# One shared PSUM pool of four double banks, score runs of up to three steps, and zero matmuls in the early gaps

## The chip, the cores and the metric

The kernel runs on one core of a Trainium2 chip. The metric is the device time of one execution in microseconds (us), median of several runs. A timed run is about 1.7 us longer than the span on its profile page.

Names of the engines: PE is TensorE (PEld its weight loads), DVE VectorE, ACT ScalarE, POOL GpSimd, SP SyncE. PSUM, into which PE writes, is used here as eight banks of 2 KiB per partition; "one bank" is 512 fp32 columns.

## The reference

Block-sparse attention (4 batches, 8 heads, 768 positions, head size 64; the mask has global blocks, a window and three random blocks per query block) is followed by a feed-forward layer with a gated activation.

```python
scores = scale * np.matmul(q, k.transpose(0, 1, 3, 2))
scores = np.where(mask, scores, -1000000000.0)
attn = np.exp(scores - max); attn = attn / sum
x = (attn @ v) as (3072, 512)
h = x @ w_in                                  # (3072, 2048)
g = h * (1.0 / (1.0 + np.exp(-beta * h)))
return g @ w_out                              # (3072, 512)
```

## The kernel before

All buffers are fixed tiles, allocated once. The order in which the instructions are issued comes from a scheduler in the kernel (`order_of`), which walks the work as nodes with modelled durations and hands out buffers. PSUM is split: two score buffers of two banks each, four one-bank buffers for all else.

```python
SLOTS = {..., "et": 15, "xst": 7, "t_sb": 5, "g": 2, "osb": 2, "sc": 2, "mm": 4}
T = {
    "sc": many(psum, "sc", [P, 2, 512], FP32),     # 2 tiles of 2 banks: scores
    "mm": many(psum, "mm", [P, 512], FP32),        # 4 tiles of 1 bank: everything else
    ...
def at(buf):
    return T[buf.pool][buf.slot]
```

A score step ("sc") is a group of 64-row matmuls that fills both banks of an `sc` tile; one exp on ACT then reads both, and DVE multiplies by the mask. The feed-forward works on units of one bank: "hp" is four matmuls into one `mm` bank, "th" a tanh on ACT that reads the bank, and "gm" a DVE operation that reads the tanh and the bank again.

```python
hb, tb = Buf("mm"), Buf("t_sb")
def hp(f=f, hb=hb):
    for c in range(NPAIR):                          # 4 matmuls of 512 columns
        nc.tensor.matmul(at(hb)[:, 0:n], lhsT=w_in_sb[:, c, f * P:(f + 1) * P],
                         rhs=xT_sb[:, c, t0:t0 + n], start=(c == 0), stop=(c == NPAIR - 1))
def th(eng, ...):
    nc.scalar.activation(out=at(tb)[:, 0:n], in_=at(hb)[:, 0:n], func=AF.Tanh, ...)
def gm(eng, ...):
    nc.vector.scalar_tensor_tensor(out=at(gb)[:, f, 0:n], in0=at(tb)[:, 0:n],
                                   scalar=1.0, in1=at(hb)[:, 0:n], op0=ALU.add, op1=ALU.mult)
...
seq = order_of(nodes, {...}, SLOTS)
with tc.manual_schedule():
    for n in seq:
        n.emit(...)
```

The kernel fixes the order; the semaphores that keep the engines apart are placed by the programming layer beneath it.

The softmax here doesn't subtract the row's maximum and nothing guards it: scores larger than these inputs give would overflow.

Of the kernel before, what the change touches and what calls it, by code (L numbers as in the profile page):

```python
# [23 lines left out]
class Node:  # L24


    def __init__(self, kind, eng, dur, lat, emit, deps=(), take=(), use=(), moved=0,
# [10 lines left out]
        self.start = self.done = self.on = None  # L38


BIAS = {"av": 39, "beta": 625, "cast": 183, "dma": -860, "ex": 395, "gm": -151, "hp": 34,
        "load": 1245, "lone sc": 160, "mask": -541, "mk": 266, "next sc": -48, "norm": 134,
        "op": 45, "op on": 85, "osb": 304, "sc": -79, "spread": 28, "th": 302, "turn": -1220,
        "turn cp": 47, "weights": 444, "x cp": 29, "x turn": -13}

W_GATE = (3, "k")
SLACK = 1500.0
AHEAD = 3
HOP = 60.0
SWITCH = 100.0  # L50
RATE = {"SP": 305.0, "POOL": 410.0}
# [2 lines left out]
SHARED = 42.0  # L54


def order_of(nodes, free, slots):

    free = dict(free)
    give = {p: [(0.0, s) for s in range(n)] for p, n in slots.items()}  # L60
    rows = 128
    wire = {"SP": 0.0, "POOL": 0.0}
    port = {"DVE": 0.0, "POOL": 0.0}
    left, after, at_dep = {}, {}, {}
    todo = []
    for n in nodes:
        left[n] = len(n.deps)
        at_dep[n] = n.at
        for d, x in n.deps:
            after.setdefault(d, []).append((n, x))  # L70
        if not n.deps:
            todo.append(n)
    out = []
    while todo:
        best = None
        for n in todo:
            ready = at_dep[n]
            want = {}
            for b in n.take:
                want[b.pool] = want.get(b.pool, 0) + 1  # L80
            ok = True
            for p, c in want.items():
                if len(give[p]) < c:
                    ok = False
                    break
                ready = max(ready, sorted(give[p])[c - 1][0])
            if not ok:
                continue
            for e in n.eng:
                n_start = max(ready, free[e])  # L90
                if n.port and e in port:
                    n_start = max(n_start, port["POOL" if e == "DVE" else "DVE"])
                bias = BIAS[n.kind]
                if n.rows == 64:
                    if rows == 64:
                        bias += BIAS["next sc"]
                    elif sum(t <= n_start for t, _ in give["sc"]) < 2:
                        bias += BIAS["lone sc"]
                key = (n_start + n.dur[e] - min(n.dur.values()) + bias, n.place)
                if best is None or key < best[0]:  # L100
                    best = (key, n, e, n_start)
        if best is None:
            raise RuntimeError("no node can start")
        _, n, e, start = best
        if e == "PE" and n.rows != rows:
            start, rows = start + SWITCH, n.rows
        n.on, n.start = e, start
        free[e] = start + n.dur[e]
        if n.port and e in port:
            port[e] = free[e]  # L110
        if n.moved:
            other = "POOL" if e == "SP" else "SP"
            t, rest, rate = max(wire[e], start + DMA_FIRST[e]), n.moved, RATE[e]
            if e == "SP" and wire[other] > t:
                both = min(rest, (wire[other] - t) * SHARED)
                wire[other] += both / RATE[other]
                t, rest = t + both / SHARED, rest - both
            wire[e] = t + rest / rate
            n.done = wire[e] + DMA_LAST
        else:  # L120
            n.done = free[e] + n.tail
        for b in n.take:
            t, b.slot = min(give[b.pool])
            give[b.pool].remove((t, b.slot))
        for b in n.use:
            b.users -= 1
            b.end = max(b.end, n.done)
            if b.users == 0:
                give[b.pool].append((b.end + HOP, b.slot))
        todo.remove(n)  # L130
        out.append(n)
        for m, x in after.get(n, ()):
            at_dep[m] = max(at_dep[m], n.done + HOP + x)
            left[m] -= 1
            if left[m] == 0:
                todo.append(m)
    if len(out) < len(nodes):
        raise RuntimeError("some nodes never become ready")
    return out


@with_exitstack
def kernel(
# [11 lines left out]
    nc = tc.nc  # L155
# [14 lines left out]
    VW = D + 2  # L170
    Q1 = 256

    SLOTS = {"st_k": 3, "st_q": 6, "st_v": 4, "s16_k": 4, "s16_q": 2, "set": 4, "va": 5,
             "et": 15, "xst": 7, "recip": 6, "t_sb": 5, "g": 2, "osb": 2, "sc": 2, "mm": 4}

    persist = ctx.enter_context(tc.tile_pool(name="persist", bufs=1))
    psum = ctx.enter_context(tc.tile_pool(name="psum", bufs=1, space=bass.MemoryType.PSUM))
# [1 line left out]
    def many(pool, tag, shape, dtype):  # L179
        return [pool.tile(shape, dtype, name=f"{tag}_{i}") for i in range(SLOTS[tag])]  # L180

    T = {
        "sc": many(psum, "sc", [P, 2, 512], FP32),
        "mm": many(psum, "mm", [P, 512], FP32),
        "et": many(persist, "et", [P, 2, 512], FP16),
        "xst": many(persist, "xst", [P, 4, 2, D], FP16),
        "recip": many(persist, "recip", [P, 2, 2, 1], FP32),
# [10 lines left out]
        T[f"s16_{nm}"] = many(persist, f"s16_{nm}", [P, 2 * NC * D], FP16)  # L198

    def at(buf):  # L200
        return T[buf.pool][buf.slot]

    identity = persist.tile([P, P], FP16, name="identity")
# [157 lines left out]
    def by_chunk(s16, lo, hi):  # L361
        return at(s16)[:, lo * P:hi * P].rearrange("p (c h d) -> p h c d", h=2, d=D)

    def add_load(nm, x, st, lo, hi, gate):
        b, j = pairs[x]
        src = {"k": k, "q": q, "v": v}[nm]

        def load():
            hg = src[b, 2 * j:2 * j + 2].rearrange("h (g p c) d -> p (h g) (c d)", g=NG, p=P)
            o = at(st).rearrange("p h (g c) -> p (h g) c", g=NG)  # L370
            if hi - lo == NC:
                nc.sync.dma_start(out=o, in_=hg)
            else:
                for g in range(lo // CG, hi // CG):
                    nc.sync.dma_start(out=o[:, g::NG], in_=hg[:, g::NG])
        deps = [(d, -1e9) for d in last_load + begin]
        kw = {"take": [st]}
        if gate is not None:
            def shut():
                nc.gpsimd.tensor_copy(out=at(st)[0:1, 0, lo * D:lo * D + 1],  # L380
                                      in_=w_out_sb[0:1, gate * 8, 0:1])
            deps.append(add("weights", "POOL", 600, 50, shut, deps=[w_out_of[gate]], take=[st]))
            kw = {"use": [st]}
        last_load[:] = [add("load", "SP", 500 if hi - lo in (NC, CG) else 1000, 0, load, deps=deps,
                             moved=68000 * (hi - lo) + (500000 if x == 0 and nm == "v" else 0),
                             **kw)]
        return last_load[0]

    def add_cast(x, nm, st, dst, lo, hi, load):
        w = (hi - lo) * P  # L390

        def cast(eng):
# [3 lines left out]
              in_=src)  # L396
        return add("cast", ("DVE", "POOL"), {"DVE": 60 + 0.53 * w, "POOL": 50 + 0.94 * w}, 90, cast,
                   deps=[(load, SLACK if x >= NPAIR else 4000 if lo and x == 3 else 0)],
                   take=[dst], use=[st], port=True)

    def add_half(x, nm, kq, lo, hi, first, gate):

        i = "kq".index(nm)
        w = (hi - lo) * P
        st, s16 = Buf(f"st_{nm}"), Buf(f"s16_{nm}")
        load = add_load(nm, x, st, lo, hi, gate)
        if x < NPAIR and lo == 0:
            loads[x, nm] = st, load
        c = add_cast(x, nm, st, s16, lo, hi, load)
        if x >= N_PE_TURN:  # L410
            def turn():
                nc.sync.dma_start_transpose(
# [18 lines left out]
    def add_prep(x, gates=(None, None, None)):  # L431
        kq, va, st = Buf("set"), Buf("va"), Buf("st_v")
        hi = Q1 // P if x < NPAIR else NC
        tk = add_half(x, "k", kq, 0, NC, None, gates[0])
        tq = add_half(x, "q", kq, 0, hi, tk, gates[1])
        lv = add_load("v", x, st, 0, NC, gates[2])
        cv = add_cast(x, "v", st, va, 0, NC, lv)
        prep[x] = {"kq": kq, "va": va, "k": tk, "q": tq, "q on": tq, "v": cv}
        if x < NPAIR:
            loads[x, "v"] = st, lv  # L440

# [6 lines left out]
    def tile_steps(x, q0, n):  # L448
# [5 lines left out]
        for kc0 in range(0, NC, kn):  # L454
# [19 lines left out]
            def mk(eng, et=et, kc0=kc0):  # L474
# [3 lines left out]
                    [P, 2 * CG * kn, w])  # L478
                nc.vector.tensor_tensor(out=e, in0=e, in1=m, op=ALU.mult)  # L479

            steps.append((x, q0, sc, et, mm, ex, mk,
                          [mask_of[g] for g in range(q0 // (CG * P), (q0 + n) // (CG * P))]))
        return steps, ets

    sc_of = {}

    def add_step(step, unit):
        x, q0, sc, et, mm, ex, mk, masks = step
        r = prep[x]
        g = add("sc", "PE", 218, 180, mm, deps=[(r["k"], SLACK if x >= N_PE_TURN else 0),  # L490
                      (r["q"] if q0 == 0 else r["q on"], SLACK if x >= N_PE_TURN else 0)],
                take=[sc], use=[r["kq"]], rows=64)
        sc_of.setdefault(unit, g)
# [136 lines left out]
    for i, (b, q0, n) in enumerate(tiles):  # L630
# [12 lines left out]
        while gi < len(moe) and moe[gi][0] + moe[gi][1] <= upto:  # L643
            add_moe(*moe[gi], gi)
            gi += 1

    seq = order_of(nodes, {"PE": 3900.0, "ACT": 3950.0, "DVE": 2800.0, "POOL": 3350.0,
                           "SP": 800.0}, SLOTS)

    with tc.manual_schedule():  # L650
        emit_first()
        for n in seq:
            if n.on in ("ACT", "DVE", "POOL") and n.emit.__code__.co_argcount > n_default(n.emit):
                n.emit(n.on)
            else:
                n.emit()
# [34 lines left out]
```

## Time and profile before

| | before |
|---|---|
| median of 3 runs | 280.38 us (280.29 to 280.6) |
| the profiled run | 281.79 us (span 280.1) |
| PE busy | 265.3 us, 95% |
| first hp matmul; second hp tile; last matmul | 33.61; 63.16; 276.05 us |

These lines are from the page of the kernel before: busy time by engine, the PE and clock rows of the forty slices, the chain of waits, and three groups. In the names, `et` is the exp of the scores, `va` the values, `xst` and `xT_sb` the attention output before and after it is turned (transposed), `t_sb` the tanh, `g` the gated activation, `osb` a piece of the result. A group's columns are its busy time and the mean ns of one instruction, then the engine's idle time before those instructions and what ended most of it.

```profile
PE 265.3 (95%) x2455; PEld 139.5 (50%) x2455; DVE 209.5 (75%) x424; ACT 212.9 (76%) x281; POOL 28.0 (10%) x45
PE   4597899999999999999999999999999999999994
PEclk9997799999999999999999999999999999999999
PE 83%; ACT 7%; DVE 4%; DMA 3%; issue 2%; SPq 0%; ACTq 0%; DVEq 0%
L567 PE MATMUL mm<-xT_sb,w_in_sb 128*128 128x512 f16 (+1 forms) x448 | 89.9, 349 | 0.4
L572 ACT ACTIVATE t_sb<-mm,beta_h_sb 128x512 f16<-128x512 f32 (+1 forms) x112 | 67.8, 649 | 12.9 <-PE mm L567 12.1
L576 DVE SCALAR_TENSOR_TENSOR g<-t_sb,mm 128x512 f16<-128x512 f16 (+1 forms) x112 | 66.0, 608 | 23.3 <-ACT t_sb L572 22.2
```

PE is the bound. ACT and DVE have slack, and they wait for PE or for one another. From the second hp tile to the last matmul PE has no gap at all; this is the window from 63.16 to 276.05 us (busy time of each engine, then clock and DMA):

```profile
63.16:276.05 212.89, 212.89 (x1884) 107.89 (x1882) 156.75 (x297) 163.06 (x214) 14.02 (x16) 1.00 0.45 109
```

What is left to gain there is the change between 128-row and 64-row matmuls. This is a piece of PE's timeline (start, duration, what, how many):

```profile
144.86 0.93 PE L517 MATMUL mm<-va,et 128*128 128x65 f16 x24
145.72 0.61 PE L462 MATMUL sc<-qX,kX 64*128 64x512 f16 x4
146.26 1.04 PE L591 MATMUL mm<-w_out_sb,g 128*128 128x512 f16 x4
```

Adding up starts between 66 and 260 us, 103 such edges cost 9.7 us, or 94 ns each. The Trainium skill ("TensorEngine Tiling (Array Packing)", Key Properties) says that a change of the tiling mode drains the TensorE; the trace fits that and gives the size that the page does not, though it does not tell a drain from any other cost of the change.

### The profile page before, as it was taken

What the parts mean: (1) busy time and instruction counts of PE and PEld (TensorE: products, weight loads), DVE (VectorE), ACT (ScalarE), POOL (GpSimd) and SP (SyncE); (2) the same over time, 40 slices, a digit from 0 to 9 for tenths busy, and PEclk for the clock granted to TensorE, in tenths of its full rate; (3) what the DMA queues carried; (4) which work ended last, traced back from release to release, by engine and by line L of the source; (5) the groups of instructions that cost most, each with busy time, mean ns of one, the idle gap of its engine ahead of it and who ended that gap; (6) DMA issues with size and microseconds to landing.
All of it is one profiled execution on the core that took longest, in us unless ns stands there. A gap on an engine that the chain in (4) does not pass through costs nothing.

```text
span 280.1 us, 6128 instructions
## 1 busy us (share of the span) xinstructions
PE 265.3 (95%) x2455; PEld 139.5 (50%) x2455; DVE 209.5 (75%) x424; ACT 212.9 (76%) x281; POOL 28.0 (10%) x45
## 2 busy tenths in 40 slices
PE   4597899999999999999999999999999999999994
PEld 1364576654363664454563354643355554556741
DVE  5697999999995788887789998877876787733500
ACT  1689898879987898997879988879966877704611
POOL 5560010010200010231001310010000000000000
PEclk9997799999999999999999999999999999999999
DMA  7999994899602194996227986860102010011112
GB/s 204 292 251 213 202 176 115 109 305 233 163 4 37 48 247 115 303 252 150 68 70 204 266 207 86 248 104 35 39 2 77 37 49 37 0 22 75 40 55 96
DMA packets 72849, 36.65 MB, mean 131 GB/s; under 512 B 29796, under 2 KB 68724, under 8 KB 72820
## 3 DMA queue, kind: packets, MB, share of 16 engines
q1 hardware_dynamic: 69568, 32.06, 47.0%
q0 software_dynamic: 3136, 4.19, 8.6%
q8 instruction: 19, 0.31, 0.5%
q14 instruction: 10, 0.08, 0.1%
q10 hardware_dynamic: 116, 0.01, 0.0%
HBM read 27.27 MB, written 6.29 MB: 120 GB/s over the span
## 4 chain that ended last, share of the span: by engine, by line
PE 83%; ACT 7%; DVE 4%; DMA 3%; issue 2%; SPq 0%; ACTq 0%; DVEq 0%
PE mm L591 29%; PE mm L567 28%; PE mm L517 12%; PE sc L462 12%; ACT et L470 5%; DMA st_k<-in_k_dram 2%; PE mm L420 1%; DMA sb_i<-in_sampled_blocks_dram 1%; DVE g L576 1%; DVE et L479 1%; ACT t_sb L572 1%; DVE s_k L395 1%; ACT qX L425 0%; DVE s_q L395 0%; ACT kX L425 0%
## 5 line engine op out<-in xcount | busy, mean ns | idle before, releaser
L470 ACT ACTIVATE et<-sc 128x1024 f16<-128x1024 f32 x144 | 142.2, 1031 | 24.7 <-PE sc L462 22.0
L479 DVE TENSOR_TENSOR et<-et,mask 128x1024 f16<-128x1024 f16 x144 | 98.6, 695 | 20.0 <-ACT et L470 19.7
L591 PE MATMUL mm<-w_out_sb,g 128*128 128x512 f16 x384 | 93.3, 380 | 0.0
L567 PE MATMUL mm<-xT_sb,w_in_sb 128*128 128x512 f16 (+1 forms) x448 | 89.9, 349 | 0.4
L576 DVE SCALAR_TENSOR_TENSOR g<-t_sb,mm 128x512 f16<-128x512 f16 (+1 forms) x112 | 66.0, 608 | 23.3 <-ACT t_sb L572 22.2
L572 ACT ACTIVATE t_sb<-mm,beta_h_sb 128x512 f16<-128x512 f32 (+1 forms) x112 | 67.8, 649 | 12.9 <-PE mm L567 12.1
L567 PEld LDWEIGHTS <-w_in_sb 128*128 128x128 f16 x448 | 42.4, 98 | 44.5 <-issue 6.8
L591 PEld LDWEIGHTS <-g 128*128 128x128 f16 x384 | 33.7, 98 | 43.6 <-issue 11.5
L462 PE MATMUL sc<-qX,kX 64*128 64x256 f16 (+1 forms) x384 | 48.4, 342 | 4.3 <-ACT et L470 3.0
L517 PEld LDWEIGHTS <-et 128*128 128x128 f16 x1152 | 42.3, 100 | 9.2 <-issue 3.1
L517 PE MATMUL mm<-va,et 128*128 128x65 f16 x1152 | 44.5, 196 | 0.0
L462 PEld LDWEIGHTS <-kX 64*128 64x128 f16 x384 | 15.5, 96 | 26.9 <-issue 21.8
L601 ACT ACTIVATE osb<-mm 128x512 f32<-128x512 f32 x16 | 9.6, 599 | 18.9 <-PE mm L591 18.7
L527 DVE TENSOR_TENSOR xst<-mm,recip 128x256 f16<-128x256 f32 x48 | 20.1, 419 | 0.4
L395 POOL CAST s_q<-st_q 128x768 f16<-128x768 f32 (+1 forms) x10 | 8.5, 847 | 92.8 <-DMA st_q<-in_q_dram 89.5
L524 DVE RECIPROCAL recip<-mm 128x4 f32<-128x4 f32 x48 | 8.5, 178 | 5.5 <-PE mm L517 4.9
L395 POOL CAST va<-st_v 128x768 f16<-128x768 f32 x7 | 6.9, 983 | 15.4 <-DMA st_v<-in_v_dram 15.4
L395 DVE CAST s_k<-st_k 128x768 f16<-128x768 f32 x12 | 7.9, 656 | 0.7 <-DMA st_k<-in_k_dram 0.7
L395 DVE CAST va<-st_v 128x768 f16<-128x768 f32 x9 | 4.9, 546 | 1.5 <-DMA st_v<-in_v_dram 1.5
L395 POOL CAST s_k<-st_k 128x768 f16<-128x768 f32 x4 | 3.5, 875 | 20.8 <-DMA st_k<-in_k_dram 20.8
L603 DVE TENSOR_SCALAR osb<-mm 128x512 f32<-128x512 f32 x8 | 5.5, 684 | 0.0
L395 DVE CAST s_q<-st_q 128x512 f16<-128x512 f32 (+2 forms) x10 | 4.5, 454 | 0.0
(53 smaller groups left out, 44.3 us busy)
## 6 DMA issues: line engine op xcount, KB each, us to landing
st_k<-in_k_dram SPq DMA_DIRECT2D x16, 384.0 KB, 4.8
st_v<-in_v_dram SPq DMA_DIRECT2D x16, 384.0 KB, 5.3
out_dram<-osb SPq DMA_DIRECT2D x24, 256.0 KB, 2.0
st_q<-in_q_dram SPq DMA_DIRECT2D x12, 384.0 KB, 4.6
w_in_sb<-in_moe_w_in_dram POOLq DMA_DIRECT2D x2, 1024.0 KB, 12.0
w_out_sb<-in_moe_w_out_dram POOLq DMA_DIRECT2D x2, 1024.0 KB, 21.2
st_q<-in_q_dram SPq DMA_DIRECT2D x12, 128.0 KB, 4.6
xT_sb<-xst SPq DMA_TRANSPOSE x22, 2.4
```

Source lines behind the costliest of these rows:

```text
L395: e(out=at(dst)[:, :, :, 0:D] if nm == "v" else by_chunk(dst, lo, hi), in_=src)
L462: nc.tensor.matmul(at(sc)[:, hh, i * n:(i + 1) * n], lhsT=kX[hh * D:(hh + 1) * D, (kc0 + i) * P:(kc0 + i + 1) * P], rhs=qX[hh * D:(hh + 1) ...
L470: nc.scalar.activation(out=at(et).rearrange("p h q -> p (h q)"), in_=at(sc).rearrange("p h q -> p (h q)"), func=AF.Exp, bias=0.0, scale=SCALE)
L479: nc.vector.tensor_tensor(out=e, in0=e, in1=m, op=ALU.mult)
L517: nc.tensor.matmul(a[:, i, hh, :], lhsT=at(ets[kc // kn])[:, hh, at0:at0 + P], rhs=at(va)[:, hh, kc, 0:D + 1], start=(kc == 0), stop=(kc = ...
L524: nc.vector.reciprocal(out=at(rb), in_=av_ap()[:, :, :, D:D + 1])
L527: nc.vector.tensor_tensor(out=at(xs)[:, half * 2:half * 2 + 2], in0=av_ap()[:, :, :, 0:D], in1=at(rb).to_broadcast([P, 2, 2, D]), op=ALU.mult)
L567: nc.tensor.matmul(at(hb)[:, 0:n], lhsT=w_in_sb[:, c, f * P:(f + 1) * P], rhs=xT_sb[:, c, t0:t0 + n], start=(c == 0), stop=(c == NPAIR - 1))
L572: nc.scalar.activation(out=at(tb)[:, 0:n], in_=at(hb)[:, 0:n], func=AF.Tanh, bias=0.0, scale=beta_h_sb[:, f:f + 1])
L576: nc.vector.scalar_tensor_tensor(out=at(gb)[:, f, 0:n], in0=at(tb)[:, 0:n], scalar=1.0, in1=at(hb)[:, 0:n], op0=ALU.add, op1=ALU.mult)
L591: nc.tensor.matmul(at(ob), lhsT=at(gb)[:, f, ts * P:(ts + 1) * P], rhs=w_out_sb[:, f, :], start=(f == 0), stop=(f == N_FFC - 1))
L601: nc.scalar.activation(out=at(sb), in_=at(ob), func=AF.Copy, bias=0.0, scale=0.5)
```

## The change

The intent: one pool of all eight banks, as four double banks. A score step takes a whole double bank, everything else takes half of one. With up to three free double banks, up to three score steps can follow each other, so there are fewer edges. Besides, the first k comes in three loads instead of one so that the first scores start earlier, and zero matmuls fill the gaps that the model sees on PE before 34 us, to keep its clock up. The scheduler's weights were tuned anew, and some buffer counts changed.

```diff
+BANKS = ("sc", "mm")
+MOST = {"av": 8, "hp": 6, "sc": 3}
+IN_PARTS = (0,)
...   (order_of keeps one list of eight banks; "sc" takes a pair, "mm" a single bank)
+                        room = sum(whole(bank, d, n_start) for d in range(len(bank) // 2))
+                        bias += BIAS["lone sc"] if room < 2 else BIAS["two sc"] if room < 3 else 0
...
-             "et": 15, "xst": 7, "recip": 6, "t_sb": 5, "g": 2, "osb": 2, "sc": 2, "mm": 4}
+             "et": 13, "xst": 5, "recip": 7, "t_sb": 6, "g": 2, "osb": 3, "sc": 4}
...
         "sc": many(psum, "sc", [P, 2, 512], FP32),
-        "mm": many(psum, "mm", [P, 512], FP32),
...
     def at(buf):
+        if buf.pool == "mm":
+            return T["sc"][buf.slot // 2][:, buf.slot % 2]
         return T[buf.pool][buf.slot]
...
+    fill = idle_fill(seq, PE_FROM)
...
+            nc.tensor.matmul(T["sc"][i // 2][:, i % 2, 0:w], lhsT=warm[0:k, 0:P],
+                             rhs=warm[0:k, 0:w], start=True, stop=True)
...
         for n in seq:
+            if n in fill:
+                emit_fill(*fill[n])
```

More of the change, by code (lines that the diff above doesn't have):

```diff
@@ L38, in __init__ @@
         self.start = self.done = self.on = None
-BIAS = {"av": 39, "beta": 625, "cast": 183, "dma": -860, "ex": 395, "gm": -151, "hp": 34,
-        "load": 1245, "lone sc": 160, "mask": -541, "mk": 266, "next sc": -48, "norm": 134,
-        "op": 45, "op on": 85, "osb": 304, "sc": -79, "spread": 28, "th": 302, "turn": -1220,
-        "turn cp": 47, "weights": 444, "x cp": 29, "x turn": -13}
+BIAS = {"av": -69, "beta": -455, "cast": 94, "dma": -1239, "ex": 257, "gm": -727, "hp": -468,
+        "load": 1496, "lone sc": 331, "mask": -1415, "mk": 241, "next sc": 94, "norm": -152,
+        "op": -13, "op on": -70, "osb": 284, "sc": -204, "spread": -316, "th": 422,
+        "turn": -3422, "turn cp": -88, "two sc": -72, "weights": 774, "x cp": -31,
+        "x turn": -102}
 W_GATE = (3, "k")
@@ L48 @@
 AHEAD = 3
+IN_PARTS = (0,)
+PE_FROM = 3900.0
+WARM_END = 34000.0
+WARM_EDGE = 150.0
 HOP = 60.0
@@ L54, with banks_of, whole, soonest @@
 SHARED = 42.0
+BANKS = ("sc", "mm")
+MOST = {"av": 8, "hp": 6, "sc": 3}
+def banks_of(b):
+    return (2 * b.slot, 2 * b.slot + 1) if b.pool == "sc" else (b.slot,)
+def whole(bank, d, t):
+    return all(x is not None and x <= t for x in bank[2 * d:2 * d + 2])
+def soonest(bank, pool):
+    if pool == "mm":
+        return min((t for t in bank if t is not None), default=None)
+    pairs = [bank[i:i + 2] for i in range(0, len(bank), 2)]
+    return min((max(p) for p in pairs if None not in p), default=None)
+def bank_for(bank, pool, t):
+    if pool == "sc":
+        ok = [d for d in range(len(bank) // 2) if whole(bank, d, t)]
+        return min(ok, key=lambda d: max(bank[2 * d:2 * d + 2]))
+    ok = [i for i in range(len(bank)) if bank[i] is not None and bank[i] <= t]
+    def other(i):
+        return float("inf") if bank[i ^ 1] is None else bank[i ^ 1]
+    return max(ok, key=lambda i: (other(i), -i))
 def order_of(nodes, free, slots):
     free = dict(free)
-    give = {p: [(0.0, s) for s in range(n)] for p, n in slots.items()}
+    give = {p: [(0.0, s) for s in range(n)] for p, n in slots.items() if p not in BANKS}
+    bank, held = [0.0] * (2 * slots["sc"]), {}
     rows = 128
@@ L81, in order_of @@
             ok = True
+            if held.get(n.kind, 0) >= MOST.get(n.kind, 99):
+                continue
             for p, c in want.items():
+                if p in BANKS:
+                    t = soonest(bank, p)
+                    if t is None:
+                        ok = False
+                        break
+                    ready = max(ready, t)
+                    continue
                 if len(give[p]) < c:
@@ L96, in order_of @@
                         bias += BIAS["next sc"]
-                    elif sum(t <= n_start for t, _ in give["sc"]) < 2:
-                        bias += BIAS["lone sc"]
+                    else:
+                        room = sum(whole(bank, d, n_start) for d in range(len(bank) // 2))
+                        bias += BIAS["lone sc"] if room < 2 else BIAS["two sc"] if room < 3 else 0
                 key = (n_start + n.dur[e] - min(n.dur.values()) + bias, n.place)
@@ L122, in order_of @@
         for b in n.take:
+            if b.pool in BANKS:
+                b.slot, b.kind = bank_for(bank, b.pool, start), n.kind
+                held[n.kind] = held.get(n.kind, 0) + 1
+                for i in banks_of(b):
+                    bank[i] = None
+                continue
             t, b.slot = min(give[b.pool])
@@ L127, in order_of @@
             b.end = max(b.end, n.done)
-            if b.users == 0:
+            if b.users == 0 and b.pool in BANKS:
+                held[b.kind] -= 1
+                for i in banks_of(b):
+                    bank[i] = b.end + HOP
+            elif b.users == 0:
                 give[b.pool].append((b.end + HOP, b.slot))
@@ L139, in order_of, with idle_fill @@
     return out
+def idle_fill(seq, free):
+    busy = [[] for _ in range(2 * 4)]
+    for n in seq:
+        for b in n.take:
+            if b.pool in BANKS:
+                for i in banks_of(b):
+                    busy[i].append((n.start, b.end + HOP))
+    fill, end, rows = {}, free, 128
+    for n in seq:
+        if n.on != "PE":
+            continue
+        if n.start > WARM_END:
+            break
+        gap = n.start - end - (SWITCH if n.rows != rows else 0)
+        cols = int((gap - WARM_EDGE) * 2.4) // 64 * 64
+        if cols > 0:
+            ok = [i for i in range(8) if all(e < end - HOP or s >= n.start for s, e in busy[i])]
+            if ok:
+                fill[n] = (rows, ok[-1], cols)
+        end, rows = n.start + n.dur["PE"], n.rows
+    return fill
 @with_exitstack
@@ L171 @@
     Q1 = 256
-    SLOTS = {"st_k": 3, "st_q": 6, "st_v": 4, "s16_k": 4, "s16_q": 2, "set": 4, "va": 5,
-             "et": 15, "xst": 7, "recip": 6, "t_sb": 5, "g": 2, "osb": 2, "sc": 2, "mm": 4}
+    SLOTS = {"st_k": 2, "st_q": 5, "st_v": 5, "s16_k": 4, "s16_q": 2, "set": 4, "va": 4,
+             "et": 13, "xst": 5, "recip": 7, "t_sb": 6, "g": 2, "osb": 3, "sc": 4}
     persist = ctx.enter_context(tc.tile_pool(name="persist", bufs=1))
@@ L362, in by_chunk, with add_load @@
         return at(s16)[:, lo * P:hi * P].rearrange("p (c h d) -> p h c d", h=2, d=D)
-    def add_load(nm, x, st, lo, hi, gate):
+    def add_load(nm, x, st, lo, hi, gate, more=False):
         b, j = pairs[x]
@@ L376, in add_load @@
         deps = [(d, -1e9) for d in last_load + begin]
-        kw = {"take": [st]}
+        kw = {"use" if more else "take": [st]}
         if gate is not None:
@@ L384, in add_load, with add_cast @@
         last_load[:] = [add("load", "SP", 500 if hi - lo in (NC, CG) else 1000, 0, load, deps=deps,
-                             moved=68000 * (hi - lo) + (500000 if x == 0 and nm == "v" else 0),
+                             moved=68000 * (hi - lo) + (170000 if x == 0 and nm == "v" else 0),
                              **kw)]
         return last_load[0]
-    def add_cast(x, nm, st, dst, lo, hi, load):
+    def add_cast(x, nm, st, dst, lo, hi, load, more=False):
         w = (hi - lo) * P
@@ L398, in add_cast, with add_half @@
                    deps=[(load, SLACK if x >= NPAIR else 4000 if lo and x == 3 else 0)],
-                   take=[dst], use=[st], port=True)
-    def add_half(x, nm, kq, lo, hi, first, gate):
+                   take=[] if more else [dst], use=[st] + ([dst] if more else []), port=True)
+    def add_half(x, nm, kq, lo, hi, first, gate, at_work=None):
         i = "kq".index(nm)
         w = (hi - lo) * P
-        st, s16 = Buf(f"st_{nm}"), Buf(f"s16_{nm}")
-        load = add_load(nm, x, st, lo, hi, gate)
+        st, s16 = at_work or (Buf(f"st_{nm}"), Buf(f"s16_{nm}"))
+        load = add_load(nm, x, st, lo, hi, gate, at_work and lo > 0)
         if x < NPAIR and lo == 0:
             loads[x, nm] = st, load
-        c = add_cast(x, nm, st, s16, lo, hi, load)
+        c = add_cast(x, nm, st, s16, lo, hi, load, at_work and lo > 0)
         if x >= N_PE_TURN:
@@ L433, in add_prep @@
         hi = Q1 // P if x < NPAIR else NC
-        tk = add_half(x, "k", kq, 0, NC, None, gates[0])
-        tq = add_half(x, "q", kq, 0, hi, tk, gates[1])
+        parts = []
+        if x in IN_PARTS:
+            work = Buf("st_k"), Buf("s16_k")
+            for g in range(NG):
+                parts.append(add_half(x, "k", kq, g * CG, g * CG + CG,
+                                      parts[0] if parts else None, None, work))
+                if g == 0:
+                    tq = add_half(x, "q", kq, 0, hi, parts[0], None)
+            tk = parts[0]
+        else:
+            tk = add_half(x, "k", kq, 0, NC, None, gates[0])
+            tq = add_half(x, "q", kq, 0, hi, tk, gates[1])
         lv = add_load("v", x, st, 0, NC, gates[2])
         cv = add_cast(x, "v", st, va, 0, NC, lv)
-        prep[x] = {"kq": kq, "va": va, "k": tk, "q": tq, "q on": tq, "v": cv}
+        prep[x] = {"kq": kq, "va": va, "k": tk, "q": tq, "q on": tq, "v": cv,
+                   "k of": parts or [tk] * NG}
         if x < NPAIR:
@@ L479, in mk @@
                 nc.vector.tensor_tensor(out=e, in0=e, in1=m, op=ALU.mult)
-            steps.append((x, q0, sc, et, mm, ex, mk,
+            k_of = prep[x]["k of"][kc0 // CG:(kc0 + kn - 1) // CG + 1]
+            steps.append((x, q0, k_of, sc, et, mm, ex, mk,
                           [mask_of[g] for g in range(q0 // (CG * P), (q0 + n) // (CG * P))]))
@@ L487, in add_step @@
     def add_step(step, unit):
-        x, q0, sc, et, mm, ex, mk, masks = step
+        x, q0, k_of, sc, et, mm, ex, mk, masks = step
         r = prep[x]
-        g = add("sc", "PE", 218, 180, mm, deps=[(r["k"], SLACK if x >= N_PE_TURN else 0),
+        g = add("sc", "PE", 218, 180, mm, deps=[(t, SLACK if x >= N_PE_TURN else 0)
+                                           for t in dict.fromkeys(k_of)] + [
                       (r["q"] if q0 == 0 else r["q on"], SLACK if x >= N_PE_TURN else 0)],
@@ L645, with emit_fill @@
             gi += 1
-    seq = order_of(nodes, {"PE": 3900.0, "ACT": 3950.0, "DVE": 2800.0, "POOL": 3350.0,
+    seq = order_of(nodes, {"PE": PE_FROM, "ACT": 3950.0, "DVE": 2800.0, "POOL": 3350.0,
                            "SP": 800.0}, SLOTS)
+    fill = idle_fill(seq, PE_FROM)
+    def emit_fill(rows, i, cols):
+        while cols > 0:
+            w = min(cols, 512)
+            k = 64 if rows == 64 else P
+            nc.tensor.matmul(T["sc"][i // 2][:, i % 2, 0:w], lhsT=warm[0:k, 0:P],
+                             rhs=warm[0:k, 0:w], start=True, stop=True)
+            cols -= w
     with tc.manual_schedule():
```

## The prediction

> **What bounds it now.** By the page, PE is busy 265.3 of 280.1 us and the chain of waits is 83% PE. In the PE timeline from 66 to 277 us PE waits for no other engine. A 128x512 matmul starts 216 ns after its neighbour. The one regular loss is at the edges of a score run (64-row matmuls): 312 ns going in, 308 going out. 103 edges between 66 and 260 us cost 9.7 us: 94 ns each, 188 ns a run, however long. The Trainium skill ("TensorEngine Tiling (Array Packing)", Key Properties) says that changing the tiling mode drains the TensorE; the trace agrees, with 94 ns an edge.
>
> Before 63 us ACT bounds. The first feed-forward (hp) matmul starts at 33.6 us, the second tile's at 63.2. Exp over 128x1024 takes 0.945 us back to back; ACT is busy 20.6 of the 24.9 us to 33.6 and 26.3 of the next 29.6. PE waits some 20 us in the first 34, partly because two score buffers hold up other PE work in order (0.94 and 0.38 us for exp at 24.9 and 25.8). The clock was granted at half from 23.0 to 29.8 us.
>
> **What moves** (counted in the order of instructions). The work is the same, 144 score steps, plus 40 zero matmuls (16,128 columns, 6.7 us at 2.4 columns/ns), all before the first hp.
> 1. Score runs go from 78 (mostly of two steps) to 57 (32 of three). From the second hp tile on, 52 become 38: 14 x 188 ns = 2.6 us, all on the critical path. Earlier ones count little, since ACT bounds there.
> 2. k in parts ahead of v, and free double banks, let exp start 0.7 us earlier and with fewer holes (ACT has 4 us of holes before 33.6 and 3 us from there to 63.2). Walking the new order with the trace's durations: first score about 7.3 us, first hp about 30, second tile 59.5 to 60.5, with 0.7 us less PE work left then.
> 3. Zero matmuls should keep the clock up at 23 to 30 us; the skill ("TensorE: Matmul & The Clock Gate", Part 1) says a window of about 3.4 us of idling halves it. PE is not the bound there: under 1 us. Some will delay real work by tenths.
> 4. Against it: hp now comes in unbroken blocks of 64, and from 60 to 100 us ACT needs about 39 of 42 us. I allow 1 us of new PE waits. Fewer k staging, et and va buffers add risk.
>
> **Sum.** 280.4 - 2.6 (runs) - 3.2 (start) - 0.7 (work done earlier) - 0.5 (small waits between 34 and 63) + 1.0 (new waits) = 273.4 us. Range 270.3 to 276.8. Faster by over 2%: 0.68; within 2%: 0.31; slower: 0.01.
>
> **What would show it.** Edges still about 94 ns, some 28 fewer from the second hp tile on; first hp at 29 to 31 us, second tile at 59 to 61; ACT's holes before 60 us down by 3 us; no half clock at 20 to 30 us; the end (last matmul to end, 3.6 us) unchanged; PE waits for exp after 60 us under 1.5 us in sum.
>
> **What would make it wrong.** The DMA stream: w_out's second half landed at 41.3 us, and the matmuls that need it now come about 42; the fifth pair's k and q must be turned by about 53. If late, PE stands still in order and the start's gain is lost. Or ACT falls behind in three-step runs, and score matmuls wait after 60 us. Or zero matmuls placed by modelled gaps push back real work. On the good side, if ACT loses no time before 60 us the start gives 5 us.

## The result, and the profile after

| | before | after |
|---|---|---|
| median | 280.34 us (4 runs, 279.56 to 280.6) | 340.12 us (4 runs, 338.67 to 340.88) |
| ratio | | 1.2132, 95% interval 1.2081 to 1.2183 |
| first hp; second hp tile; last matmul | 33.61; 63.16; 276.05 us | 37.94; 79.19; 334.49 us |

A ratio here is the mean time of one kernel's fast runs over that of the other's in the same rounds, so it is not quite the ratio of the medians quoted.

The kernel is 21% slower. These lines of the page of after answer to those of before:

```profile
PE 281.4 (83%) x2495; PEld 145.1 (43%) x2495; DVE 208.9 (62%) x416; ACT 216.7 (64%) x284; POOL 31.7 (9%) x53
PE   7977857976769898788899989897789898887884
PEclk9997999999997999999999999999999999999998
PE 62%; DVE 19%; ACT 13%; issue 3%; POOL 1%; ACTq 0%; DVEq 0%; POOLq 0%
L664 PE MATMUL sc<-xT_sb,w_in_sb 128*128 128x512 f16 (+1 forms) x448 | 89.9, 348 | 19.7 <-DVE g L673 18.5
L669 ACT ACTIVATE t_sb<-sc,beta_h_sb 128x512 f16<-128x512 f32 (+1 forms) x112 | 66.6, 624 | 55.3 <-PE sc L664 31.7
L673 DVE SCALAR_TENSOR_TENSOR g<-t_sb,sc 128x512 f16<-128x512 f16 (+1 forms) x112 | 66.0, 610 | 51.4 <-ACT t_sb L669 51.0
L753 PE MATMUL sc<-warm 128*128 128x512 f16 (+9 forms) x40 | 12.5, 436 | 2.8 <-DVE xT_sb L642 1.7
```

The work itself has not grown: the hp matmuls are busy for 89.9 us in both. It is the waits that are new. The hp matmuls now wait 19.7 us instead of 0.4, tanh 55.3 instead of 12.9, g 51.4 instead of 23.3. The chain of waits is no longer PE alone, but runs through DVE (19%) and ACT (13%).

The zero matmuls come to 12.5 us of PE's busy time, so PE's 281.4 us are not all useful. From the second hp tile to the last matmul (the same stretch of work as shown of before, less what was done earlier):

```profile
79.19:334.49 255.30, 219.99 (x1869) 109.51 (x1869) 155.06 (x291) 161.50 (x211) 16.12 (x19) 0.99 0.38 90
```

255.3 us against 212.9, at practically full clock. So PE is idle for 35.3 us of it. The four largest of its waits in this window, from the list of waits (us in total, times, longest):

```profile
PE sc L664 <- DVE g L673: 15.4, 29, 1.2
PE sc L688 <- DVE xst L624: 5.3, 8, 0.9
PE sc L688 <- ACT osb L698: 3.5, 5, 0.7
PE sc L614 <- DVE osb L700: 3.1, 4, 0.8
```

The same list of before has one line (an exp, 0.3 us, which ends just before its window). The pattern is best seen in the timeline of after at the second hp tile (start, duration, what, and in brackets the idle time before it and what ended that):

```profile
81.11 0.69 ACT L669 ACTIVATE t_sb<-sc,beta_h_sb 128x512 f16<-128x512 f32 x1 [1.73 <-PE sc L664]
81.83 0.69 DVE L673 SCALAR_TENSOR_TENSOR g<-t_sb,sc 128x512 f16<-128x512 f16 x1 [0.40 <-ACT t_sb L669]
82.55 1.26 ACT L669 ACTIVATE t_sb<-sc,beta_h_sb 128x512 f16<-128x512 f32 x2 [0.75 <-DVE g L673]
83.27 1.29 DVE L673 SCALAR_TENSOR_TENSOR g<-t_sb,sc 128x512 f16<-128x512 f16 x2 [0.76 <-ACT t_sb L669]
84.01 1.89 PE L664 MATMUL sc<-xT_sb,w_in_sb 128*128 128x512 f16 x8 [1.21 <-DVE g L673]
84.59 0.69 ACT L669 ACTIVATE t_sb<-sc,beta_h_sb 128x512 f16<-128x512 f32 x1 [0.78 <-DVE g L673]
85.31 0.69 DVE L673 SCALAR_TENSOR_TENSOR g<-t_sb,sc 128x512 f16<-128x512 f16 x1 [0.75 <-ACT t_sb L669]
85.94 0.69 ACT L669 ACTIVATE t_sb<-sc,beta_h_sb 128x512 f16<-128x512 f32 x1 [0.66 <-PE sc L664]
```

It is a ladder: the tanh at 81.11, the g at 81.83, the tanh at 82.55, the g at 83.27, each starting when the one before it ends. The tanh at 82.55 waited for a g, though no tanh needs a result of g. Its own matmuls, the second four of sixteen that PE began at 79.19 us, 216 ns apart, were done at about 80.9. In the kernel before no tanh waits for g anywhere in the list of waits; in after 33 do, for 22.1 us.

**The reading, theory T.** Two units of hp now lie in the two halves of one tile. The built program tells which semaphore each instruction waits for, and the value; each such wait can be followed to the instruction that raises the semaphore to that value. Counted so, waits between two engines whose named accesses touch only different banks of the same tile number 0 in before and 208 in after (47 of them a tanh of one bank waiting for the hp matmuls of the other, 29 a PE write waiting for a DVE read of the other bank). Another 47, nearly all of them tanh after g, were set apart because both sides name a small tile, `t_sb`, as well. That was too careful: in a recount of the rebuilt program, buffer by buffer, only 6 of the 255 share another buffer besides the double tile, so 249 come from the banks alone, the tanh after g of the ladder among them. (The 189 of e1 below become 233 in the same way; before keeps its 0.) The layer that places the semaphores thus keeps the engines apart by tile, in program order, even a read after a read, as tanh after g; while a tile was a bank (or was used whole, like the old `sc`), that gave no such wait.

Rivals: the new order and the smaller buffer counts (O), and the zero matmuls with what they push back (Z).

### The profile page after: what moved, and what is told of

Its sections match the earlier page's. It is cut to its first block, busy times and chain, and to the rows that moved or that the text cites. A ratio compares the mean times of both kernels' runs of the same rounds, so it can differ in the third digit from the quotient of the medians.

```text
span 339.2 us, 6204 instructions
## 1 busy us (share of the span) xinstructions
PE 281.4 (83%) x2495; PEld 145.1 (43%) x2495; DVE 208.9 (62%) x416; ACT 216.7 (64%) x284; POOL 31.7 (9%) x53
## 4 chain that ended last, share of the span: by engine, by line
PE 62%; DVE 19%; ACT 13%; issue 3%; POOL 1%; ACTq 0%; DVEq 0%; POOLq 0%
PE sc L688 25%; PE sc L664 15%; PE sc L614 11%; DVE g L673 10%; ACT t_sb L669 10%; PE sc L557 7%; DVE xst L624 4%; PE sc L753 3%; ACT et L565 2%; DVE et L574 2%; ACT osb L698 2%; DVE recip L621 1%; DVE osb L700 1%; PE sc L504 1%; DVE xT_sb L642 1%
## 5 line engine op out<-in xcount | busy, mean ns | idle before, releaser
L664 PE MATMUL sc<-xT_sb,w_in_sb 128*128 128x512 f16 (+1 forms) x448 | 89.9, 348 | 19.7 <-DVE g L673 18.5
L688 PE MATMUL sc<-w_out_sb,g 128*128 128x512 f16 x384 | 93.0, 383 | 11.6 <-DVE xst L624 6.1
L669 ACT ACTIVATE t_sb<-sc,beta_h_sb 128x512 f16<-128x512 f32 (+1 forms) x112 | 66.6, 624 | 55.3 <-PE sc L664 31.7
L673 DVE SCALAR_TENSOR_TENSOR g<-t_sb,sc 128x512 f16<-128x512 f16 (+1 forms) x112 | 66.0, 610 | 51.4 <-ACT t_sb L669 51.0
L614 PE MATMUL sc<-va,et 128*128 128x65 f16 x1152 | 43.5, 195 | 11.3 <-DVE g L673 3.7
L698 ACT ACTIVATE osb<-sc 128x512 f32<-128x512 f32 x18 | 10.8, 600 | 27.4 <-PE sc L688 18.1
L621 DVE RECIPROCAL recip<-sc 128x4 f32<-128x4 f32 x48 | 8.6, 179 | 27.0 <-PE sc L614 9.5
L624 DVE TENSOR_TENSOR xst<-sc,recip 128x256 f16<-128x256 f32 x48 | 20.4, 424 | 1.8 <-DVE recip L621 0.2
L753 PE MATMUL sc<-warm 128*128 128x512 f16 (+9 forms) x40 | 12.5, 436 | 2.8 <-DVE xT_sb L642 1.7
L479 POOL CAST s_q<-st_q 128x768 f16<-128x768 f32 (+2 forms) x11 | 9.0, 814 | 43.7 <-DMA st_q<-in_q_dram 37.9
```

Source lines behind the costliest of these rows:

```text
L479: e(out=at(dst)[:, :, :, 0:D] if nm == "v" else by_chunk(dst, lo, hi), in_=src)
L614: nc.tensor.matmul(a[:, i, hh, :], lhsT=at(ets[kc // kn])[:, hh, at0:at0 + P], rhs=at(va)[:, hh, kc, 0:D + 1], start=(kc == 0), stop=(kc = ...
L624: nc.vector.tensor_tensor(out=at(xs)[:, half * 2:half * 2 + 2], in0=av_ap()[:, :, :, 0:D], in1=at(rb).to_broadcast([P, 2, 2, D]), op=ALU.mult)
L688: nc.tensor.matmul(at(ob), lhsT=at(gb)[:, f, ts * P:(ts + 1) * P], rhs=w_out_sb[:, f, :], start=(f == 0), stop=(f == N_FFC - 1))
L698: nc.scalar.activation(out=at(sb), in_=at(ob), func=AF.Copy, bias=0.0, scale=0.5)
L753: nc.tensor.matmul(T["sc"][i // 2][:, i % 2, 0:w], lhsT=warm[0:k, 0:P], rhs=warm[0:k, 0:w], start=True, stop=True)
```

## The experiments

All outputs are right. "Before" in each row is the kernel before, run on the same chip in the same rounds.

| run | median us (range) | ratio to before, 95% interval |
|---|---|---|
| e1_pairs | 355.98 (354.31 to 356.73) | 1.2646 [1.2598, 1.2694] |
| e2_perbank | 277.0 (276.13 to 279.99) | 0.9865 [0.9804, 0.9927] |
| e3_pairs_free | 281.13 (280.39 to 282.21) | 0.9985 [0.9949, 1.0021] |
| e4_nofill | 337.38 (336.29 to 340.31) | 1.2009 [1.1942, 1.2077] |
| e5_perbank_nofill | 276.66 (275.83 to 278.38) | 0.9857 [0.9820, 0.9894] |
| e7_perbank_neither | 281.59 (280.03 to 281.9) | 1.0013 [0.9983, 1.0043] |
| e8_perbank_data | 280.22 (276.8 to 282.33) | 0.9927 [0.9875, 0.9978] |
| e9_onekload | 275.63 (275.12 to 275.97) | 0.9822 [0.9802, 0.9843] |
| e10_fill_again | 276.58 (275.97 to 279.74) | 0.9886 [0.9844, 0.9927] |
| e11_nofill_again | 276.49 (275.52 to 276.96) | 0.9846 [0.9823, 0.9869] |
| e12_data_again | 280.38 (one run, state unknown) | none |

The medians of before beside them were 280.9 (e1 to e4), 280.74 (e5, e7, e8) and 280.66 (e9 to e12).

### e1: the kernel before, its one-bank tiles declared as halves

Nothing but the declaration differs from before. The order of instructions on every engine, the banks' users and the work stay.

```diff
-        "mm": many(psum, "mm", [P, 512], FP32),
+    mm2 = [psum.tile([P, 2, 512], FP32, name=f"mm_{i}") for i in range(SLOTS["mm"] // 2)]
+    T["mm"] = [mm2[i // 2][:, i % 2] for i in range(SLOTS["mm"])]
```

> The kernel before with one edit: its four one-bank PSUM tiles are declared as two tiles of two banks, of which each is used half by half. The instructions stand in the same order on every engine, only semaphore waits are added (189 waits name an access to the other bank alone; before has none). Theory T (a two-bank tile makes different engines wait for each other across its two banks): clearly slower, 300 to 345 us, with DVE g waiting for ACT tanh and PE hp waiting for DVE g, as in the changed kernel. Rival O (the new order, unbroken hp blocks and three-step runs, starves PE): no change, 280 us within 1. Rival Z (zero matmuls placed wrongly): no change, 280 us.

Measured: 355.98 us, 26% slower than before, and worse than the change itself. The two lines below are from its list of waits; of the first, before has no case.

```profile
PE mm L569 <- DVE g L578: 27.8, 28, 2.1
ACT t_sb L574 <- DVE g L578: 9.7, 14, 1.3
```

T is confirmed, though I had put the size too low. Neither O nor Z is in this kernel, so neither is needed for a loss of this size. The declaration alone adds 75 us. By my first count of waits it has 189 across banks, where before has none.

### e2: the change, with those waits taken away

The order is that of after, zero matmuls included. For each pair of instructions on different engines that touch the same double tile but no common bank, and overlap in no other tile, the layer is told that there is no dependency.

```diff
+def per_bank(tc, tiles, traced):
+    ...   (for each instruction i, the banks that it touches in each tile of `tiles`)
+            for j, other, jw, jr in old:
+                if j.engine == i.engine:
+                    continue
+                if not other & banks and not (meet(wr, jw + jr) or meet(rd, jw)):
+                    tc.declare_no_dep(i, j, reason="another bank of the same tile")
...
+    traced = []
+    nc.push_inst_callback(traced.append)
     (the loop that emits the instructions)
+    per_bank(tc, {x.tensor.name for x in T["sc"]}, traced)
```

> The changed kernel with the same order on every engine; only waits between accesses to different banks of one tile are taken away (checked free of races). Theory T: 270 to 277 us, that is, the predicted gain appears. Rival O: 330 us or more, since the order is the same. Rival Z: 320 us or more, since the zero matmuls are the same.

Measured: 277.0 us, ratio 0.9865. O had asked for 330 us or more and Z for 320: both fall. By the count no wait that comes from the banks alone is left. The 59.8 us that the change had lost all came back, and nearly 4 more. Its page, its timeline at the second hp tile and its window from there to the last matmul:

```profile
L700 PE MATMUL sc<-xT_sb,w_in_sb 128*128 128x512 f16 (+1 forms) x448 | 84.6, 349 | 0.2 <-ACT et L601 0.2
```

```profile
65.17 0.69 ACT L705 ACTIVATE t_sb<-sc,beta_h_sb 128x512 f16<-128x512 f32 x1
66.04 0.69 ACT L705 ACTIVATE t_sb<-sc,beta_h_sb 128x512 f16<-128x512 f32 x1 [0.18 <-PE sc L700]
66.90 0.69 ACT L705 ACTIVATE t_sb<-sc,beta_h_sb 128x512 f16<-128x512 f32 x1 [0.18 <-PE sc L700]
66.92 3.20 DVE L709 SCALAR_TENSOR_TENSOR g<-t_sb,sc 128x512 f16<-128x512 f16 x5
```

```profile
64.01:273.61 209.60, 209.51 (x1872) 108.07 (x1870) 158.07 (x293) 163.80 (x212) 16.18 (x19) 1.00 0.47 111
```

The ladder is gone: tanh follows PE at 0.86 to 0.87 us, the time of four hp matmuls, and does not ask for g. PE's wait before hp is 0.2 us. (The busy sum of 84.6 us is below 89.9 because some matmul records are missing from a trace.) The new order is thus good: it does the same stretch in 209.6 us where before needs 212.9. By the total, though, e2 is within 2% of before, which counts as the same here.

The correct result is also a statement about the chip. The Trainium skill ("PSUM — Partial Sum Buffer", PSUM bank collisions raise a hardware error) says that two engines on one bank and quadrant collide, on different banks "run clean", and to guard by bank and quadrant. e2 and e3 agree: by their traces, matched with the built programs, an ACT and a DVE instruction ran at once on the two banks of one double tile 47 times in e2 and 31 times in e3 (and matmuls beside one of them, hundreds of times), never on the same bank, and all results are correct. The waits of after were stricter than that rule.

### e3: the counterpart, e1 with its waits taken away

The edit is e1's and e2's together.

> Control: e1_pairs with the waits across banks taken away by the same means. Theory T: 280 us within 1.5. If it is the placement in PSUM rather than the waits that costs in e1_pairs, it stays as slow as e1_pairs.

Measured: 281.13 us, ratio 0.9985, that is before again. So it was the waits, and nothing else in the pairing of banks, that cost e1 its 75 us.

### e4: the change without zero matmuls

```diff
-    fill = idle_fill(seq, PE_FROM)
+    fill = {}
```

> The changed kernel without its 40 zero matmuls; everything else stays. Rival Z: most of the loss goes, under 300 us. Theory T: 332 to 342 us, since the zero matmuls stand only before the first hp; they cost at most the 6 us that their streaming takes.

Measured: 337.38 us. The zero matmuls are worth some 3 us of a loss of 60: Z falls as the cause here too.

### e5 and e11: per bank, without zero matmuls

The edits of e2 and e4 together; e11 is the same kernel once more, beside a repeat of e2.

> e2_perbank (277.0 us) without its 40 zero matmuls. In its profile eight of them stream at half clock from 9.3 to 12.6 us in front of the turning of the second k, which has been cast since 9.9 us, and ACT has a hole of 2 us. Theory F (the zero matmuls took what the start should have gained): first hp before 31.5 us (33.1 there), second hp tile before 62.5 us (64.0 there), total 273.5 to 275.5 us. Rival C (they are needed for the clock): half clock shows again between 16 and 34 us, the first hp does not come earlier and the time is 277 us or more. Rival D (the DMA stream and the casts set the start): 276 to 277.5 us, no change.

> e5_perbank_nofill word for word, on the same chip as e9 and e10: 276 to 277 us.

Measured: 276.66 and 276.49 us. The profile of e5 has the first hp matmul at 29.83 us and the second hp tile at 60.62, about where the prediction had put them. Theory F thus holds for the start in that profile, but the total does not: it lies over F's 273.5 to 275.5, in the range that rival D (no change) had named, and the medians of e2 and e5 are alike (277.0 and 276.66). Why shows in e10, next. Rival C falls: the half clock that e11 shows from 20.8 to 24.2 us did no visible harm (first hp at 30.28 us).

### e10: e2 once more

> e2_perbank word for word, to be compared with e11 on the same chip: whether the zero matmuls cost (theory F) or help. The profile of e2 was its slowest run (279.99 us against 276.1 to 277.4 in the others), so its late start may not be the rule. F: 0.5 to 2.5 us slower than e11. If they do nothing: within 0.4 us.

Measured: 276.58 us, but the six runs fall into two groups: 279.08 and 279.74 in two, 275.97 to 276.69 in the others. e2 had the same: 279.99 once, 276.13 to 277.38 in three. So the medians of e10 and e11 are alike, and the means differ by 1.0 us (277.4 and 276.4): F by the mean alone. In e2 and in e10 the profile is of one of the slower runs. PE in e10, and below it in e8 (next), where the run was fast:

```profile
9.31 3.30 PE L789 MATMUL sc<-warm 64*128 64x512 f16 x8
12.54 0.82 PE L540 MATMUL sc<-identity,s_k 128*128 128x128 f16 x6
```

```profile
9.11 1.73 PE L790 MATMUL sc<-warm 64*128 64x512 f16 x8
10.77 0.51 PE L541 MATMUL sc<-identity,s_k 128*128 128x128 f16 x6
```

The same eight zero matmuls take 3.30 us in the one and 1.73 in the other, because PE is still at half clock there (the clock records begin with full speed at 16.6 us in e10, at 8.0 in e8). The kernel sized them for full clock (its code divides by 2.4 columns per ns). Real work behind them waits in order: the second k is turned (transposed on PE) only from 12.54 us, and ACT stands still:

```profile
13.62 0.37 ACT L545 COPY qX<-sc 128x256 f16<-128x256 f16 x1 [2.05 <-PE sc L540]
```

In e10's profile the first hp then starts at 33.07 us, in e11's at 30.28. So zero matmuls cost some 3 us in the runs in which the clock comes late, and in the others no gain shows (276.0 to 276.7 against e11's 275.5 to 277.0). A late clock alone does not do it: in e5, without zero matmuls, full speed comes at 16.7 us as in e10, and the first hp starts at 29.83. That the quicker runs of e10 are those with an early clock is inferred from e8 and e12, two profiles of one kernel (below): full speed at 8.0 and 17.4 us, first hp at 30.62 and 33.66, total 276.95 and 280.38 us. No quick run of e10 itself was profiled.

### e8 and e12: does the data of the zero matmuls set the clock?

Counting numbers instead of zeros, in the kernel of e2:

```diff
-        nc.vector.memset(warm, 0.0)
+        nc.gpsimd.iota(warm, pattern=[[1, 512]], base=0, channel_multiplier=3,
+                       allow_small_or_imprecise_dtypes=True)
```

> e2_perbank with counting numbers instead of zeros in the operand of the warming matmuls (order and sizes the same). In all profiles so far matmuls run at half speed until 15 to 18 us, with zero matmuls or without. If zeros do not count as activity for the clock, full clock should come by 8 us here, and the time fall by 1 to 2 us; if the data does not matter, the full clock comes at 14 to 18 us as before and the time stays at 277 us within 1.

> e8_perbank_data word for word, a second profile: in the first, full clock came at 8.0 us, in the eight other profiles at 14.8 to 18.2 us. If the data in the warming matmuls does it, full clock comes before 10 us again; if it was chance, at 14 to 18 us.

Measured: e8 fell into the same two groups (276.8 and 276.95; 280.2 to 280.24 in three; one run of 282.33 counts as slow). In its profile, one of the two quicker runs, the trace's clock records begin with full speed at 8.0 us; that looked like a success. The repeat, e12, took 280.38 us, with full clock only at 17.4 us and the eight matmuls at 3.29 us. The data does not do it; e8 had been lucky. One profile of a bimodal kernel proves nothing about its cause.

### e7: per bank, the first k whole, no zero matmuls

```diff
-IN_PARTS = (0,)
+IN_PARTS = ()
```

> e5 with the first k loaded whole as in the kernel before, so of the change only the shared pool with its order is left (per bank). If k in parts is worth the 0.7 us that I took for it, about 0.5 to 1.5 us slower than e5; if it is worth nothing, within 0.5 us of it. The order shifts somewhat, since the schedule is made anew for it.

Measured: 281.59 us, ratio 1.0013: 4.9 us over e5, outside both forecasts. This run tells less than I hoped. The scheduler ordered everything anew: its second hp tile starts at 59.72 us, earlier than e5's, but from there to the last matmul it takes 216.07 us against e5's 209.48. PE's waits are 3.5 us of that (before hp at about 109 and 154 us, among others). So it does not show what the three loads are worth.

### e9: e5 in the same order, the first k in one load

```diff
+            if nm == "k" and x in IN_PARTS:
+                if lo == 0:
+                    nc.sync.dma_start(out=o, in_=hg)
```

> e5_perbank_nofill with the first k brought in by one load instead of three; the three casts, turns and copies and the order on PE, ACT, DVE and POOL stay as they are (e7 moved them too, and so does not tell). If the earlier first part is worth what I predicted (0.7 us), 0.3 to 1.2 us slower than the repeat of e5 in this call, with the first score about 1 us later; if the later k and q loads set the pace anyway, within 0.3 us.

Measured: 275.63 us, 0.9 us under e11 beside it. The order on PE, ACT, DVE and POOL is the same, so the three loads gain nothing. The first score does come later (7.23 against 6.19 us), but the first hp does not (29.29 against 30.28). And the end is shorter: from the start of the last matmul to the end of the span it is 4.01 us in e9, and 4.69 in e11. All eight profiles with three k loads (after, e2, e4, e5, e8, e10, e11, e12) have 4.66 to 4.70 there, all five without (before, e1, e3, e7, e9) 4.01 to 4.07. The built programs and the traces show most of the cause. The DMAs share eight semaphores in turn, and at the end SP waits for all eight in a fixed order of seven instructions. With two loads more, the last output store falls on the first of these: in e5 SP passes the first wait at 3.38 us after the start of the last matmul and the seventh only at 3.78. In e9 six of the seven pass while the store is still under way, and the last at 3.12. That is 0.4 us; the other 0.25 is that the store lands later (3.35 to 3.38 against 3.10 to 3.14 us), and why stays open.

e9 has the lowest median, 1.8% under before (the same, at 2%) and 19% under after; its interval overlaps that of e11.

## Why the prediction was wrong

The prediction was 273.4 us with slower at 0.01; measured was 340.12. The step that failed is the fourth: "I allow 1 us of new PE waits", with "free double banks" taken as a pure gain in step 2. In their place, the profile of after shows 27.3 us of PE waits between 79 and 334 us in the four lines above alone (35.3 in all), and a ladder between ACT and DVE that draws the whole second part out from 212.9 to 255.3 us. Another 16 us are lost before it: the second hp tile starts at 79.19 us, against 63.16 before and 64.01 in e2. e1 shows that the declaration of the tiles alone does it, e2 and e3 that taking the waits away undoes it. I had compared the order of instructions on each engine, and that is sound; but the order does not show the semaphores. The waits in the built program were there to be counted before any run, 208 by my first count against none. None of the risks that I named (DMA late, ACT behind, zero matmuls in the way) was the cause. Nor did my markers catch it: "PE waits for exp after 60 us under 1.5 us" came true in after (0.9 us), because PE waited for g and for the copies instead.

With the waits taken away, the terms can be tested one by one.

- **Fewer edges (-2.6) and less work left (-0.7).** Right. From the second hp tile on, before's profile has 52 score runs and e2's 38, as predicted, and in e2 an edge still costs 94 ns (18 edges between 150 and 200 us: 1.69 us). Second hp tile to last matmul: 212.89 us before, 209.60 in e2, 209.48 in e5. That is 3.4 us against the 3.3 predicted, and the new waits that I set against it (+1.0) are next to nothing.
- **Earlier start (-3.2).** Nearly right without zero matmuls: 29.83 and 60.62 us in e5 against "about 30" and "59.5 to 60.5", that is 2.5 us of the 3.2. With them, in the slower runs, it is lost again: 33.11 and 64.01 in e2. The three k loads, which I credited with part of it, have no share (e9). What is left is the order and, perhaps, the clock, which was at half for 6.8 us of before's start and not in e5; no run separates these two.
- **Zero matmuls (under 1 us, some tenths lost).** Right that they gain nothing, wrong in what they can cost: about 3 us in some runs. Their 6.7 us were worked out at full clock; by the pages they are busy for 10.2 us in e8, with its early clock, and 12.5 to 12.9 in the others. Two readings of before in the prediction were also off: by the trace's records the half-clock stretch is 25.0 to 31.8 us, not 23.0 to 29.8, and PE is idle for 10.4 us up to 33.6, not some 20. In after and e2 there is no half clock from 20 to 30 us, as predicted, but e5, without zero matmuls, has none either, and e11 only from 20.8 to 24.2.
- **The end unchanged.** Wrong by 0.6 to 0.7 us, in each kernel with three k loads (see e9).
- **The sum.** It has a slip of its own: 280.4 - 2.6 - 3.2 - 0.7 - 0.5 + 1.0 is 274.4, not 273.4. And its base is wrong. Terms read from a profile belong on the profiled run, which took 281.79 us with part of its start at half clock, not on the median of 280.38. Finally, the 0.5 us for small waits before 63 us is counted twice, since it is already in the start of the second tile. Put right, 281.79 - 3.2 - 2.6 - 0.7 + 1.0 gives 276.3 us. The profiled run of e5, the change per bank without zero matmuls, took 276.54. (Errors of up to 1 us here cancel. From before's profile to e5's, the start gives 2.5 us, the stretch to the last matmul 3.4, and the end takes 0.7: the start gained less, the waits were fewer, the end was longer.)

What remains open is why declared halves cost e1 more (75 us) than after (60 us). Part can be the clock: its records in e1 show half speed from 27.6 to 37.9 us and four times more for 3.4 us, in after twice for 3.4 us. Part can be which work shares a pair. No run separates the two.

## What to carry to other kernels

Before buffers are merged into larger ones, find out what the layer that places semaphores takes as its unit: here it was the tile, so independent halves of one tile became a chain over three engines, and 277 us became 340. An unchanged order of instructions proves nothing about waits; count the waits between engines in the built program, before and after. And take a prediction's terms from the run whose profile they were read in, do the sum twice, and size any filler work for the clock that it will really meet.

## What the Trainium skill lacked or had wrong

- "PSUM — Partial Sum Buffer", PSUM bank collisions raise a hardware error: gives the bank and quadrant as the unit to guard by, and the runs agree (e2, e3 correct). It lacks the warning that the programming layer may guard by whole tiles, and what that costs: 340.12 us against 277.0 in the same order, 355.98 against 281.13 in the old one.
- "TensorE: Matmul & The Clock Gate", Part 1: full clock after about 3.4 us of sustained work. Here the trace's clock records first show full speed at 14.0 to 18.2 us in the profiles, save e8's, at 8.0 us. In before, with its gaps, a late release is no surprise. But in e2 PE's timeline has no wait from 3.85 us on (PE busy 4.00 of 4.00 us from 8 to 12, and again from 12 to 16), and its matmuls still ran at half speed at 13.4 us (three of 512 columns in 1.38 us). The time of release also varies from run to run of one kernel (8.0 and 17.4 us in e8 and e12), with totals 3 us apart where zero matmuls stand in the way; the page calls the ramp under 1% of a typical span, and here 3 of 277 us is just over that. The same part says that a window of about 3.4 us of idling halves the clock, on which step 3 of the prediction rests. The length fits: the eleven half-clock stretches between 20 us and the end last 3.4 us, or two or three times that. But none of them follows 3.4 us of idling: in the 3.4 us before each, PE was busy for 1.3 to 2.1 us, and its longest single gap was 2.1 us (e1; 0.94 us in before).
- "TensorEngine Tiling (Array Packing)", Key Properties: says that a change of mode drains the TensorE, without a size. Here a change costs 94 ns an edge, between 64-row and 128-row matmuls of 512 or 65 columns.
- No page that I read has this: the stretch from the last matmul to the end of the span was 4.66 to 4.70 us in eight profiles with two DMA loads more, 4.01 to 4.07 in five without. Some 0.4 us of it is the order in which SP waits for the eight DMA semaphores at the end (see e9); the rest is a later landing, whose cause is not shown.
